# Spectral filter and Mish layer on one core: filter rows of both halves in one transfer, twelve DMA-transposed tiles in pairs, a new order

## The chip, the core and the metric

The kernel runs on one core of one Trainium2 chip. The core has a matrix engine (PE; its weight loads are shown as PEld), two elementwise engines (ACT, which is ScalarE, and DVE, which is VectorE), GpSimd (POOL) and SyncE (SP), which here only issues transfers (DMAs). Sixteen DMA engines move the data. The metric is the device time of one execution in microseconds (us).

## What is computed

The inputs are bf16. `x` has 2048 rows of 512; `B_x` is not used, both branches read the same `x`.

```python
g = sigmoid((x * gate_w).sum(-1))                 # one number a row
X = rfft2(x) * (A_w_r + 1j * A_w_i)               # filter: 2048 x 257
a = irfft2(X)                                     # 2048 x 512
h = x @ w1 + b1                                   # 512 -> 1792
b = (h * tanh(softplus(h))) @ w2                  # Mish, 1792 -> 512
out = g * a + (1 - g) * b
```

## The kernel before

The work is a list of named tasks. `_build` creates them with what they read and write, and the string `ORDER` gives every task's place: a token is the task's name, its engine and, for results in PSUM or in a temporary, the bank or slot. `_Graph.place` turns `ORDER` into one list for each engine and adds the waits; each engine then executes its list strictly in order. SP and ACT issue the DMAs that stand in their lists, also in order, and a DMA whose data is not there yet holds up all that stand behind it.

Rows of `x` are split in 16 tiles `t` of 128, and the tiles in four chunks `c` of 512 rows. These are the tasks, with the names that the texts use (line numbers are those of the kernel before):

- `x0`, `x2`, `x4`, `x8`, `x12` load `x` in five pieces (L515-516). `tr` transposes a tile on PE (L554), `evx` copies it out of PSUM into `xT`. Tiles 0 to 7 go this way; tiles 8 to 15 come transposed from DRAM by one DMA each, `xt8` to `xt15` (L533-534).
- `m{c}_{ft}` is the first matmul of the Mish layer: chunk `c`, 128 of its 1792 columns, four 512-wide matmuls (L800); `h{c}_{ft}` is its Mish on ACT (L805). The result of chunk 0 and 1 goes to `hs01`, of chunk 2 into `rD` and of chunk 3 into `rS`. So `h2` may not write `rD` before all eight DMAs `sh` have read it, and `h3` may not write `rS` before the filter has been read from there (`dph`, L791).
- `n{t}_..` is the second matmul of tile `t` (L828, 14 matmuls).
- The forward transform: `bf` sums and differences on DVE (L567), `p` on PE (L577) and its copy `ep`, `d` (L591) and its copy `ed` into `y1` in `rD`; then eight DMAs `sh0_0` to `sh1_3` (256 KB each) carry `y1` to `In` in `rE`. `sh0` needs `ed0` to `ed3`, `sh1` needs `ed4` to `ed7`. `t0` to `t7` transform `In` with the constants `ldM` (L676), with copies `et` into `Y`; `t0` to `t3` read `sh0`, `t4` to `t7` read `sh1`.
- The filter: the rows of `A_w_r` (`wr`) and `A_w_i` (`wi`) are loaded into the staging buffer `rS`. Each of the two has two halves of 32 frequencies: `wr0`, `wr1`, `wi0`, `wi1`. The plain rows of a half are one transfer of 16 rows of 16,448 bytes (`wr0s0`, 257 KB), its mirrored rows another (`s1`, 16 x 31 or 16 x 32 rows of 514 bytes), and a single row of the first half comes by itself (`s2`). `wrm`/`wim` copy from `rS` into the filter `rW` and `rA` (L638 to L641), `wrn` is a DMA that doubles the real part.
- `p2`, `p1`, `ad` on DVE multiply `Y` by the filter; `e1`, `xp`, `ead`, `e2`, `e3` treat the edge frequencies.
- The inverse transform: `it` (L750) with copies `eit`, eight DMAs `hx`, `id` (L774) with `ec` and `ey`, and `ip` (L812).
- `o` and `s` combine the branches (L817, L822), `out` DMAs store two tiles at a time; the last tile is cut at column 384.
- `gt` on DVE is the row sum for the gate, sixteen times 128x512 (L599).

The lines that make the filter's transfers and the transposing DMAs are these:

```python
parts = [(0, slice(0, 32), slice(32 * fh, 32 * fh + 32), 257), ...]      # plain rows of half fh
dma(f"{nm}{fh}s{j}", sg[pm:32:2, fs, :], wv[:, ms, :].rearrange("q m k -> q (m k)"), ...)
dma(f"xt{t}", xT[:, t // 4, :, t % 4, :], xv[:, t, :], queue=("sp",), transpose=True, ...)
```

Of the kernel before, what the change touches and what calls it, by code (L numbers as in the profile page):

```python
# [300 lines left out]
cRF:act ones:pool ident:pool ebase:pool x0:sp x2:sp w1_0a:sp warm:pe:0 fl0:pe:1  # L301
tr0:pe:0 gwl:act braw:act w1_0b:sp x4:sp bf0_0:dve bf0_1:dve tab:act w1_4:sp
x8:sp tr1:pe:1 evx1:act evx0:dve p0:pe:2 p1:pe tr2:pe:0 w1_9:sp x12:sp
wr0s1:sp wi0s2:sp wi0s0:sp wr0s2:sp cFD:sp wr0s0:sp ldM0:sp bf2_0:dve bf2_1:dve
tr3:pe:1 p2:pe:4 p3:pe tr_b:pe:6 evx3:dve ev_b:dve evx2:act fl1:pe:7 m0_2a:pe:1
m0_1a:pe:0 m0_1b:pe m0_2b:pe m0_3a:pe:6 m0_0a:pe:7 m0_3b:pe m0_0b:pe ep2:act ep0:dve
h0_2:act h0_1:act h0_3:act gwb:pe:0 bf4_0:dve bf4_1:dve tr4:pe:1 evx4:dve p4:pe:2
tr7:pe:6 p5:pe evx7:dve ep4:dve tr5:pe:4 m0_6:pe:1 tr6:pe:6 h0_0:act evx5:act
evx6:dve m0_8:pe:4 bf8_1:dve bf8_0:dve xt8:sp xt9:sp xt10:sp h0_8:act h0_6:act
gwe:act xt11:sp gt0:dve p6:pe:2 m1_8:pe:6 p7:pe p8:pe:4 p9:pe ep8:dve  # L310
ep6:act h1_8:act m0_7:pe:1 h0_7:act m1_7:pe:0 m1_5:pe:2 h1_5:act p10:pe:4 p11:pe
m1_0:pe:1 ep10:act h1_0:act bf12_1:dve bf12_0:dve gt1:dve p14:pe:2 p12:pe:6 p15:pe
p13:pe m1_4:pe:4 m0_4:pe:1 gt2:dve ep12:dve gt3:dve ep14:act d6:pe:2 d14:pe:6
gt4:dve h1_7:act h1_4:act h0_4:act ldM1:sp d7:pe gt5:dve d2:pe:4 d15:pe
ed3:act ed7:act d3:pe m1_12:pe:1 d4:pe:2 ed1:dve gt6:dve d5:pe m1_3:pe:0
ed2:dve h1_12:act h1_3:act d0:pe:4 d1:pe ed0:act m1_1:pe:1 sh0_2:sp sh0_0:sp
sh0_1:sp sh0_3:sp m1_2:pe:0 d10:pe:2 h1_2:act d12:pe:4 d13:pe h1_1:act m0_10:pe:6
d11:pe d8:pe:0 d9:pe h0_10:act ed4:act ed6:act wrm011:dve gt7:dve m2_6:pe:7
gt8:dve m1_13:pe:6 gt9:dve ed5:dve wrm000:dve gt10:dve m0_12:pe:0 m0_5:pe:1 m1_10:pe:4
gt11:dve gt12:dve t1_0:pe:2 wi0s1:sp sh1_2:sp sh1_3:sp sh1_0:sp sh1_1:sp h1_13:act  # L320
t1_1:pe m2_0:pe:6 h0_5:act wrm001:act et1:act m1_9:pe:1 m2_4:pe:5 h1_9:act gt13:dve
gt14:dve h0_12:act h1_10:act t0_0:pe:2 gt15:dve wip0:pool wip1:pool wim000:dve zcl:dve
t0_1:pe wi1s0:sp wr1s0:sp et0:act m0_9:pe:1 ez:pool wrm010:dve wr1s1:sp wi1s1:sp
m1_11:pe:0 wrp0:pool wrp1:pool m2_8:pe:4 h1_11:act h2_8:act wim011:dve wim001:dve wim010:dve
t3_0:pe:2 t3_1:pe et3:act h2_4:act h2_6:act m1_6:pe:0 m2_7:pe:4 h2_0:act h2_7:act
h0_9:act h1_6:act xt12:sp xt13:sp ez1:dve win0:dve wic0:dve wiz0:dve xt14:sp
xt15:sp wrn00:sp wrn01:sp t2_0:pe:2 t2_1:pe p20_0:dve:0 et2:dve wim110:dve m2_1:pe:5
m2_13:pe:7 h2_1:act h2_13:act ldM3:sp ldM2:sp m2_2:pe:4 m2_10:pe:1 w2_4:sp h2_10:act
h2_2:act wrm110:dve p22_0:dve:1 wim101:dve wrm101:act w2_0:sp w2_9:sp p23_0:dve:2 wim111:dve
wim100:dve wrm111:dve p22_1:dve m2_3:pe:5 m0_13:pe:7 m2_12:pe:4 m2_5:pe:6 m2_9:pe:1 p20_1:dve  # L330
m3_0:pe:0 wrn11:sp wrm100:act wrn10:sp win1:dve h0_13:act h2_12:act h2_3:act h2_9:act
h3_0:act m3_4:pe:2 m3_10:pe:7 m3_12:pe:3 m3_5:pe:1 m0_11:pe:0 m3_13:pe:5 wic1:dve wiz1:pool
wrc0:dve wrz0:dve p23_1:dve h2_5:act h3_4:act h3_5:act h3_10:act h3_12:act h3_13:act
m3_3:pe:1 m3_9:pe:3 t5_0:pe:4 h3_3:act h0_11:act t5_1:pe t4_0:pe:6 t4_1:pe m3_11:pe:2
t6_0:pe:0 t6_1:pe p1_3:dve p1_0:dve ad_0:dve et5:act et4:act h3_9:act m2_11:pe:4
m3_2:pe:5 p21_0:dve:0 h3_11:act p21_1:dve p1_1:dve p1_2:dve ad_2:dve t7_0:pe:2 m3_7:pe:6
t7_1:pe m3_1:pe:7 h2_11:act et6:act ad_3:dve omg:dve ad_1:dve p24_0:dve:1 p25_0:dve:0
p25_1:dve p26_0:dve:2 p24_1:dve p26_1:dve m3_6:pe:4 h3_7:act et7:act wrc1:dve wrz1:dve
n2_0:pe:6 n1_0:pe:2 gc:dve p1_6:dve p1_4:dve o1_0:act n6_0:pe:3 o6_0:act h3_1:act
# [12 lines left out]
ip11:pe:2 ip5:pe:4 id0:pe:6 id1:pe s15_384:dve n13_0:pe:5 ec8:act:0 s5:dve ey8_0:dve
ey8_1:dve ec0:act:1 out15_384:sp ey0_0:dve ey0_1:dve id2:pe:0 id3:pe ip10:pe:4 ip14:pe:6
o14:dve out5:sp n14_0:pe:7 o10:act o11:dve s11_0:dve s13_0:dve ip6:pe:6 n10_0:pe:5
ip1:pe:4 ec2:act:0 ey2_0:dve s14_0:dve ey2_1:dve ip3:pe:7 ip2:pe:0 ip9:pe:1 ip8:pe:3
n8_0:pe:2 s10_0:dve s1:dve s6:dve o9:act out11:act s3:dve s2:dve out3:act
ip7:pe:0 ip0:pe:1 o8:dve s0:dve s7:dve out1:act out7:act n9_0:pe:3 s9_0:dve
s8_0:dve out13:sp out14:sp out9:sp n15_0:pe:0 s15_0:dve out15_0:act
# [3 lines left out]
def _build(nc, A_x, A_w_r, A_w_i, B_x, B_w1, B_b1, B_w2, gate_w, out, XTP=8, LATE=8, NWARM=13, TRM=4,  # L362
# [10 lines left out]
    with es:  # L373
# [41 lines left out]
        xT = rX[:].rearrange("p (c a t m) -> p c a t m", c=NCH, a=4, t=4)  # L415
# [106 lines left out]
        for ri, (src, nm) in enumerate(((A_w_r, "wr"), (A_w_i, "wi"))):  # L522
            wv = src.rearrange("(q m) k -> q m k", m=128)
            for fh in range(2):
                sg = stg[64 * ri + 32 * fh:64 * ri + 32 * fh + 32]
                c0_ = 1 - fh
                parts = [(0, slice(0, 32), slice(32 * fh, 32 * fh + 32), 257),
                         (1, slice(31, 0, -1) if fh == 0 else slice(31, None, -1), slice(97, 128) if fh == 0 else slice(65, 97), 514)]
                if fh == 0:
                    parts.append((1, slice(0, 1), slice(64, 65), 8))  # L530
                for j, (pm, fs, ms, kb) in enumerate(parts):
                    dma(f"{nm}{fh}s{j}", sg[pm:32:2, fs, :], wv[:, ms, :].rearrange("q m k -> q (m k)"), kb=kb, writes=[(nm, fh, "s", j)])
        for t in range(XTP, NT):  # L533
            dma(f"xt{t}", xT[:, t // 4, :, t % 4, :], xv[:, t, :], queue=("sp",), transpose=True, kb=128, writes=[("xT", t)])
# [9 lines left out]
        for t in range(XTP):  # L544
            b = _Buf("b1")

            def f_tr(e, t=t, b=b):
                ins = None
                for dt_ in range(4):
                    xs = x_sb[:, t, 128 * dt_:128 * (dt_ + 1)]  # L550
                    if t < TRM:
                        ins = e.matmul(bank(b)[:, 128 * dt_:128 * (dt_ + 1)], xs, identt[:, :], start=True, stop=True)
                    else:
                        ins = e.transpose(bankb(b)[:, 128 * dt_:128 * (dt_ + 1)], xs, identt[:, :])  # L554
# [3 lines left out]
            evac(f"evx{t}", lambda t=t: xT[:, t // 4, :, t % 4, :], lambda b=b, t=t: (bank(b) if t < TRM else bankb(b)[:, 0:512]).rearrange("p (a c) -> p a c", a=4), 512, [b], [("xT", t)], "trm" if t < TRM else "tr")  # L558
        for t in range(XTP, NT):
# [230 lines left out]
        for c in range(NCH):  # L790
            dph = {0: [], 1: [], 2: t_sh, 3: t_mv}[c]  # L791
            for ft in range(NFT):
# [3 lines left out]
                for h in ((0, 1) if split else (2,)):  # L796
                    def f_mm1(e, c=c, ft=ft, b=b, h=h):
                        ins = None
                        for dt_ in (range(4) if h == 2 else range(2 * h, 2 * h + 2)):
                            ins = e.matmul(bank(b), w1_sb[:, dt_, 128 * ft:128 * (ft + 1)], xT[:, c, dt_, :, :], start=(dt_ == 0), stop=(dt_ == 3))  # L800
# [98 lines left out]
```

## Time and profile before

| | us |
|---|---|
| median of 3 runs (130.64 to 131.45) | 130.84 |
| the profiled execution | 130.94 |
| its span, from the first to the last instruction | 129.2 |
| outside the span | 1.7 |

The profile shows one execution. PE's clock was granted in full throughout. A row of the chain of waits or of the timeline begins with its start and its length in us; "x34" is how many instructions were merged into it. SPq and ACTq rows are issues of DMAs. The list of DMA issues has, last in each row, the median us from issue to landing. In the 40 slices each digit is the busy share of 3.2 us in tenths.

### The profile page before, as it was taken

The page shows a single profiled execution, that of the slowest core. Times are in us where ns is not written, and L with a number is a line of the kernel's source. Part 1 is how long each engine was busy: PE and PEld are TensorE (multiplying, and loading weights), DVE is VectorE, ACT ScalarE, POOL GpSimd, SP SyncE. Part 2 cuts the span into 40 slices and gives each one's busy share as a digit, 9 for nine tenths or more (in the row PEclk, how much of TensorE's full clock was granted, in tenths as well). Part 3 has the DMA queues.
Part 4 walks back from the last instruction along what each step waited for, and adds up shares of the span by engine and source line. Part 5 has one row for each costly group of instructions (what it writes and reads, how often), then busy time and mean ns, then how long its engine had stood idle before and what let it go on. Part 6 is the DMA issues. An engine that isn't in the chain of part 4 may idle for free.

```text
span 129.2 us, 2150 instructions
## 1 busy us (share of the span) xinstructions
PE 124.5 (96%) x841; PEld 68.1 (53%) x856; DVE 95.6 (74%) x164; ACT 71.8 (56%) x101; POOL 5.8 (5%) x13
## 2 busy tenths in 40 slices
PE   7999999999999999999999999998999999999992
PEld 5645656765555544346544447583556554544450
DVE  0748699999997999999799833463196679677851
ACT  3556689979799999999930275273015331302000
POOL 2000000000077000000000000000000000000000
PEclk9999999999999999999999999999999999999999
DMA  3999999919999999999159200004902002032243
GB/s 89 308 334 396 251 209 138 252 51 327 296 271 155 183 219 338 360 266 228 41 134 274 119 0 0 0 5 154 391 33 77 9 0 91 0 122 81 81 167 112
DMA packets 16759, 21.20 MB, mean 164 GB/s; under 512 B 5805, under 2 KB 11694, under 8 KB 16686
## 3 DMA queue, kind: packets, MB, share of 16 engines
q1 hardware_dynamic: 15280, 18.84, 55.8%
q10 hardware_dynamic: 1470, 2.23, 4.7%
q8 instruction: 7, 0.11, 0.4%
q14 instruction: 2, 0.02, 0.0%
HBM read 12.66 MB, written 2.10 MB: 114 GB/s over the span
## 4 chain that ended last, share of the span: by engine, by line
PE 88%; DMA 3%; ACT 3%; DVE 1%; ACTq 1%; issue 1%; SPq 0%
PE ps L800 36%; PE ps L828 35%; DMA rA<-in_A_x_dram 3%; PE ps L750 3%; PE ps L676 3%; PE ps L591 3%; PE ps L774 3%; PE ps L812 3%; PE ps L577 2%; ACTq L463 1%; ACT hs L805 1%; ACT rF L475 1%; PE ps L554 1%; ACT rC L475 1%; DVE rB L567 1%
## 5 line engine op out<-in xcount | busy, mean ns | idle before, releaser
L800 PE MATMUL ps<-rX,w_sb 128*128 128x512 bf16 x215 | 50.3, 379 | 0.5
L800 PEld LDWEIGHTS ps<-rX,w_sb 128*128 128x128 bf16 x224 | 20.7, 98 | 21.9 <-ACT rD L805 1.1
L828 PE MATMUL ps<-w_sb,hs 128*128 128x512 bf16 x109 | 24.9, 379 | 0.6 <-ACT rX L817 0.4
L805 ACT ACTIVATE hs<-ps,b1f 128x512 bf16<-128x512 f32 x28 | 18.4, 697 | 5.0 <-PE ps L800 4.9
L828 PEld LDWEIGHTS ps<-w_sb,hs 128*128 128x128 bf16 x112 | 10.8, 98 | 13.0 <-ACT rX L817 0.9
L828 PE MATMUL ps<-w_sb,rS 128*128 128x512 bf16 (+2 forms) x70 | 12.9, 336 | 0.0
L828 PE MATMUL ps<-w_sb,rD 128*128 128x512 bf16 x55 | 12.5, 379 | 0.1
L599 DVE SCALAR_TENSOR_TENSOR w_sb<-rA,w_sb 128x512 bf16<-128x512 bf16 x16 | 11.0, 688 | 1.4 <-ACT w_sb L475 1.0
L689 DVE TENSOR_TENSOR tmp<-rC,rA 64x1024 bf16<-64x1024 bf16 x16 | 10.7, 685 | 1.1 <-ACT rC L475 0.6
L475 ACT ACTIVATE rC<-ps 128x1024 bf16<-128x1024 f32 x11 | 11.2, 1034 | 0.3 <-PE ps L577 0.3
L817 ACT ACTIVATE rX<-ps,omg 128x512 bf16<-128x512 f32 x5 | 3.4, 687 | 13.7 <-PE ps L828 12.0
L784 DVE TENSOR_TENSOR rA<-tmp,ps 128x512 bf16<-128x512 f32 x16 | 10.1, 679 | 1.3 <-ACT tmp L475 1.2
L567 DVE TENSOR_TENSOR rB<-rA 128x1024 bf16<-128x1024 bf16 (+1 forms) x10 | 5.4, 580 | 5.7 <-DMA rA<-in_A_x_dram 5.5
L475 ACT ACTIVATE tmp<-ps 128x512 f32<-128x512 f32 x7 | 4.1, 595 | 9.6 <-PE ps L774 9.6
L828 PEld LDWEIGHTS ps<-w_sb,rS 128*128 128x128 bf16 x70 | 6.3, 98 | 5.6
L822 DVE SCALAR_TENSOR_TENSOR rX<-ps,omg,rX 128x512 bf16<-128x512 f32 (+2 forms) x9 | 6.0, 688 | 4.1 <-PE ps L828 4.0
L805 ACT ACTIVATE rD<-ps,b1f 128x512 bf16<-128x512 f32 x14 | 8.9, 717 | 0.3 <-PE ps L800 0.3
L805 ACT ACTIVATE rS<-ps,b1f 128x512 bf16<-128x512 f32 x14 | 8.8, 721 | 0.3 <-PE ps L800 0.3
L828 PEld LDWEIGHTS ps<-w_sb,rD 128*128 128x128 bf16 x56 | 5.5, 98 | 6.6 <-DVE rX L822 0.2
L817 ACT ACTIVATE rX<-ps,gcol 128x512 bf16<-128x512 f32 x4 | 2.6, 686 | 9.2 <-PE ps L812 6.2
L475 DVE CAST rF<-ps 128x1024 bf16<-128x1024 f32 x4 | 4.8, 1222 | 3.8 <-PE ps L750 3.8
L822 DVE SCALAR_TENSOR_TENSOR rX<-ps,gcol,rX 128x512 bf16<-128x512 f32 x8 | 5.6, 745 | 2.3 <-PE ps L812 2.3
(78 smaller groups left out, 132.3 us busy)
## 6 DMA issues: line engine op xcount, KB each, us to landing
w_sb<-in_B_w_dram SPq DMA_DIRECT2D x4, 640.0 KB, 9.6
rF<-c_m SPq DMA_DIRECT2D x4, 512.0 KB, 6.6
rE<-rD SPq DMA_DIRECT2D x8, 256.0 KB, 2.6
rB<-c_g SPq DMA_DIRECT2D x4, 512.0 KB, 6.4
rA<-in_A_x_dram SPq DMA_DIRECT2D x3, 512.0 KB, 9.1
rW<-rW SPq DMA_DIRECT2D x4, 260.0 KB, 7.5
rC<-rF ACTq DMA_DIRECT2D x4, 256.0 KB, 3.3
rC<-rF SPq DMA_DIRECT2D x4, 256.0 KB, 3.7
```

The lines of the kernel that those rows point to most:

```text
L475: fns = dict(dve=lambda e: e.tensor_copy(out=o(), in_=i()), act=lambda e: e.activation(o(), i(), AF.Copy))
L567: return e.tensor_tensor(out=xu[:, a:b_, uv, :], in0=x_sb[:, a:b_, 0:256], in1=x_sb[:, a:b_, 256:512], op=ALU.add if uv == 0 else ALU.subt ...
L591: ins = e.matmul(o[:, 2 * e_:2 * e_ + 2, uv, :], zu[:, c, g, :], FD[:, c, :].rearrange("p (r k) -> p r k", r=2), start=True, stop=True)
L599: t_gt.append(dve(f"gt{t}", "gate", "stt", 512, lambda e, t=t: e.scalar_tensor_tensor(out=junk, in0=x_sb[:, t, :], scalar=1.0, in1=gwr, op ...
L676: ins = e.matmul(bank(b, i)[:, 128 * k:128 * (k + 1)], Mm[:, f, :], In[:, _fin(f), :], start=True, stop=True)
L689: return e.tensor_tensor(out=zv(z)[lo], in0=Y[hi, f0:f0 + 8, :], in1=Wi[hi, f0:f0 + 8, 0:128], op=ALU.mult)
L784: return e.tensor_tensor(out=yb[:, t:t + 2, 256 * h:256 * h + 256].rearrange("p t (i e) -> p t i e", e=2), in0=t4(z), in1=o4(bank(b, 1)), ...
L800: ins = e.matmul(bank(b), w1_sb[:, dt_, 128 * ft:128 * (ft + 1)], xT[:, c, dt_, :, :], start=(dt_ == 0), stop=(dt_ == 3))
L805: G.add(f"h{c}_{ft}", "mish", dict(act=lambda e, c=c, ft=ft, b=b: e.activation(hs[c][:, ft, :], bank(b), AF.Mish, bias=b1f[:, ft:ft + 1])) ...
L817: f_a = lambda e: e.activation(o_()[0], o_()[1], AF.Copy, scale=o_()[2])
L822: dve(name, "fin", "psums", hi - lo, lambda e: e.scalar_tensor_tensor(out=bs[:, t, lo:hi], in0=bank(b)[:, 0:hi - lo], scalar=col[:, t:t + ...
L828: ins = e.matmul(bank(b)[:, 0:hi - lo], hs[c][:, ft, 128 * tl:128 * (tl + 1)], w2_sb[:, ft, lo:hi], start=(ft == 0), stop=(ft == NFT - 1))
```

## The change

- `XTP` falls from 8 to 4: tiles 4 to 15 are transposed by DMA, two tiles in one transfer of 256 KB (`xt4`, `xt6`, ... `xt14`), so there are six such DMAs instead of eight, and `tr4` to `tr7` with their copies are gone. The layout of `xT` becomes tile before column block; the first matmul reads it with that stride.
- The plain rows of both halves come in one transfer each, `wis0` and `wrs0`: on the SBUF side 32 partitions of 16,448 bytes, on the DRAM side a pattern of 2 x 16 rows of 16,448 bytes (the half is the outer count). The single rows become `wis2` and `wrs2` in the same way (2 x 16 rows of 514 bytes). The mirrored rows stay, now 31 in both halves.
- All outputs are issued by ACT. The last tile's 128 columns are computed last, where before the 384 were.
- `ORDER` is written anew: engines, banks and places. The gate's broadcast copy `gwe` goes to DVE and `ep0` to ACT; more `hx` go to SP; five `n` instead of four stand ahead of `it`.

```diff
-... XTP=8, LATE=8, NWARM=13, TRM=4,
+... XTP=4, LATE=8, NWARM=13, TRM=4,
-        xT = rX[:].rearrange("p (c a t m) -> p c a t m", c=NCH, a=4, t=4)
+        xT = rX[:].rearrange("p (c t a m) -> p c t a m", c=NCH, a=4, t=4)
+            wh = src.rearrange("(q a h f) k -> a h q f k", a=2, h=2, f=32)
+            sg = stg[64 * ri:64 * ri + 64]
+            dma(f"{nm}s0", sg[0:64:2].rearrange("p f k -> p (f k)"), wh[0].rearrange("h q f k -> h q (f k)"), kb=514, ...)
+            dma(f"{nm}s2", sg[1:64:2, 0, :], wh[1][:, :, 0, :], kb=16, ...)
             for fh in range(2):
-                parts = [(0, slice(0, 32), slice(32 * fh, 32 * fh + 32), 257), ...]
-                for j, (pm, fs, ms, kb) in enumerate(parts):
-                    dma(f"{nm}{fh}s{j}", sg[pm:32:2, fs, :], wv[:, ms, :].rearrange("q m k -> q (m k)"), kb=kb, ...)
-        for t in range(XTP, NT):
-            dma(f"xt{t}", xT[:, t // 4, :, t % 4, :], xv[:, t, :], queue=("sp",), transpose=True, kb=128, ...)
+                ms = slice(97, 128) if fh == 0 else slice(65, 96)
+                dma(f"{nm}{fh}s1", sg[32 * fh + 1:32 * fh + 32:2, 31:0:-1, :], wv[:, ms, :].rearrange("q m k -> q (m k)"), kb=249, ...)
+        for t in range(XTP, NT, 2):
+            dma(f"xt{t}", xT[:, t // 4, t % 4:t % 4 + 2, :, :].rearrange("p t a m -> p (t a) m"), xv[:, t:t + 2, :].rearrange("p t d -> p (t d)"),
+                queue=("sp",), transpose=True, kb=256, ...)
-                            ins = e.matmul(bank(b), w1_sb[:, dt_, 128 * ft:128 * (ft + 1)], xT[:, c, dt_, :, :], ...)
+                            ins = e.matmul(bank(b), w1_sb[:, dt_, 128 * ft:128 * (ft + 1)], xT[:, c, :, dt_, :], ...)
```

Of the new order these places matter to the prediction. The first is SP's list around the redistribution `sh` (the rows `rE<-rD`); `rS` rows are the filter's, `c_m` is `ldM`, and the transposes are `xt`. Before:

```order
L463 DMA rF<-c_m 128x2048
L463 DMA rE<-rD 128x1x1024 [waits s_dve,s_act]
L463 DMA rE<-rD 128x1x1024 x3
L463 DMA rS<-in_A_w_i_dram 16x31x257
L463 DMA rE<-rD 128x1x1024 [waits s_dve,s_act]
L463 DMA rE<-rD 128x1x1024 x3
L463 DMA rS<-in_A_w_i_dram 16x8224
L463 DMA rS<-in_A_w_r_dram 16x8224
L463 DMA rS<-in_A_w_r_dram 16x32x257
L463 DMA rS<-in_A_w_i_dram 16x32x257
L462 DMA_TRANSPOSE rX<-in_A_x_dram 128x4x128 x4
```

The same place in the changed kernel, where its rows are numbered one line lower in the code:

```order
L462 DMA rE<-rD 128x1x1024 x2
L462 DMA rS<-in_A_w_i_dram 32x1x257
L462 DMA rS<-in_A_w_i_dram 32x1x8224
L462 DMA rS<-in_A_w_r_dram 16x31x257
L462 DMA rS<-in_A_w_r_dram 32x1x257
L462 DMA rS<-in_A_w_r_dram 32x1x8224
L462 DMA rE<-rD 128x1x1024 [waits s_act,s_dve]
L462 DMA rE<-rD 128x1x1024 x3
L462 DMA rS<-in_A_w_r_dram 16x31x257
L461 DMA_TRANSPOSE rX<-in_A_x_dram 128x8x128 x2
```

The two merged transfers (`32x1x8224`) and three smaller ones now stand between the last of `sh0` and the first of `sh1`, where before stood only one transfer of mirrored rows.

The second is ACT's list around the first `h2`, the row that waits for all eight `sh`; `hs` rows are `h0` and `h1`, `rC` rows are `et`, `rD` rows are `h2`. Before:

```order
L475 ACTIVATE rC<-ps 128x1024 [waits s_pe]
L805 ACTIVATE hs<-ps,b1f 128x512 [waits s_pe]
L805 ACTIVATE rD<-ps,b1f 128x512 [waits d_sh1_1,d_sh1_0,d_sh1_2,d_sh0_3,d_sh1_3,d_sh0_2,s_pe,d_sh0_1,d_sh0_0]
L475 ACTIVATE rC<-ps 128x1024 [waits s_pe]
L805 ACTIVATE rD<-ps,b1f 128x512 x3
L805 ACTIVATE rD<-ps,b1f 128x512 [waits s_pe]
```

In the changed kernel:

```order
L474 ACTIVATE rC<-ps 128x1024 [waits s_pe]
L474 ACTIVATE rC<-ps 128x1024
L803 ACTIVATE rD<-ps,b1f 128x512 [waits d_sh1_1,d_sh1_0,d_sh1_2,d_sh0_3,d_sh1_3,d_sh0_2,s_pe,d_sh0_1,d_sh0_0]
L803 ACTIVATE rD<-ps,b1f 128x512
L803 ACTIVATE rD<-ps,b1f 128x512 [waits s_pe]
L803 ACTIVATE rD<-ps,b1f 128x512
L803 ACTIVATE rD<-ps,b1f 128x512 [waits s_pe] x2
L803 ACTIVATE rD<-ps,b1f 128x512
L636 ACTIVATE rA<-rS 32x16x129 [waits d_wi1s1,d_wis2,d_wis0,s_dve]
```

All copies `et` of `t0` to `t3` now stand ahead of the first `h2`, seven `h2` follow in a row, and a copy of the filter stands on ACT behind them.

More of the change, by code (lines that the diff above doesn't have):

```diff
@@ L300 @@
 ORDER = """
[L301 to L327, printed above, removed]
@@ L627, in _build @@
                 sg = stg[64 * ri + 32 * fh:64 * ri + 32 * fh + 32]
-                rd = [(nm, fh, "s", j) for j in range(3 - fh)]
+                rd = [(nm, fh, "s", j) for j in range(3)]
                 mv = []
```

108 lines of the change are left out of this document (65 added, 43 removed).

## The prediction

> **What bounds the kernel now.** I read the page's first two parts, then the chain of waits in order of time, then the timelines of SP and ACT and the list of DMA issues.
>
> ```profile
> PE 124.5 (96%) x841; PEld 68.1 (53%) x856; DVE 95.6 (74%) x164; ACT 71.8 (56%) x101; POOL 5.8 (5%) x13
> PE   7999999999999999999999999998999999999992
> DMA  3999999919999999999159200004902002032243
> GB/s 89 308 334 396 251 209 138 252 51 327 296 271 155 183 219 338 360 266 228 41 134 274 119 0 0 0 5 154 391 33 77 9 0 91 0 122 81 81 167 112
> PE 88%; DMA 3%; ACT 3%; DVE 1%; ACTq 1%; issue 1%; SPq 0%
> ```
>
> PE has no idle slice between the first and the last, and the chain lies on it for 88%. So a saving is worth only what it takes off PE's list, off the start or off the tail. Against that, every wait that holds PE's list up costs in full. The second thing to see is the DMA row: the sixteen engines are busy almost without a break up to slice 18, some 61 us. A transfer that comes late there has no slack behind it.
>
> The chain also gives PE's pace, free of overlap:
>
> ```profile
> 7.08 3.40 PE ps L800 x15
> 11.97 0.22 PE ps L554 x4
> 34.63 0.45 PE ps L676 x8
> 43.32 7.34 PE ps L800 x34
> 126.82 0.62 DVE rX L822
> ```
>
> A 512-wide matmul is 7.34 / 34 = 0.216 us, a 128-wide one 0.45 / 8 = 0.056 us, a transpose the same. The last PE work ends at 126.8.
>
> **The change, part by part.** *Transposes.* `tr4` to `tr7` are 16 of the 0.056 us rows: PE loses 0.9 us. Their copies lie on ACT and DVE beside other work and go for nothing. What was their cover goes too: before, `m1` could start as soon as tiles 4 to 7 were transposed on PE. Now `m1` needs `xt4` and `xt6`, and these queue behind `x12`. Two rows of DVE's timeline show when the third and the last piece of `x` (`x4`, `x12`) came, since `bf4` and `bf12` start on them:
>
> ```profile
> 9.78 1.29 DVE L567 TENSOR_TENSOR rB<-rA 128x1024 bf16<-128x1024 bf16 x2 [1.63 <-DMA rA<-in_A_x_dram]
> 17.94 1.29 DVE L567 TENSOR_TENSOR rB<-rA 128x1024 bf16<-128x1024 bf16 x2
> ```
>
> SP's first nine issues are the same in both kernels, so `x4` and `x12` come at the same times. In the new list PE can do, from the end of `bf4` at 9.78 + 1.29 = 11.1: six `m0` and eight `p`, 24 x 0.216 + 32 x 0.056 = 7.0 us, to 18.1. The next is `p14`, which needs `bf12` on DVE, 17.94 + 1.29 = 19.2. So PE waits 1.1 us there; before, `m1_0` stood in that place.
>
> *Issue of the pairs.* SP's own time for the transposes:
>
> ```profile
> 13.10 9.60 SPq L462 DMA_TRANSPOSE rX<-in_A_x_dram  x4
> 37.50 5.57 SPq L462 DMA_TRANSPOSE rX<-in_A_x_dram  x4
> ```
>
> A tile takes 1.4 us to issue where nothing holds it up, 2.4 us where the queue ahead is full. A pair should take 2.8 to 4.8. The four pairs begin at about 11 us, the second is out by 20.5 (it can't be out before `x12` and `wi1s1` drain), and lands at about 22. `m1_1` is reached at 24, so I cost this at nothing; if a pair took the 4.8 after 18 us, `xt6` would land at 25 to 26, and PE would wait 2.
>
> *Outputs and the tail.* The last `s` goes from 384 columns (0.62 above) to 128 columns, and its store from 96 to 32 KB:
>
> ```profile
> L822 DVE SCALAR_TENSOR_TENSOR rX<-ps,omg,rX 128x128 bf16<-128x128 f32 x1 | 0.4, 351 | 0.0
> out_dram<-rX ACTq DMA_DIRECT2D x1, 96.0 KB, 1.7
> out_dram<-rX SPq DMA_DIRECT2D x1, 32.0 KB, 1.5
> ```
>
> That is 0.27 + 0.2, so 0.5 us less. ACT issues the stores when it has nothing else left, so its issue time is covered.
>
> *The merged filter rows.* This is the term that decides. SP's list now has `sh0`, then `wis2`, `wis0`, `wr0s1`, `wrs2`, `wrs0`, then `sh1`. What a transfer costs depends on how many DMA engines share it. The list of DMA issues tells something of that:
>
> ```profile
> w_sb<-in_gate_w_dram ACTq DMA_DIRECT2D x1, 1.0 KB
> w_sb<-in_B_b_dram ACTq DMA_DIRECT2D x1, 3.5 KB
> rS<-in_A_w_i_dram SPq DMA_DIRECT2D x3, 257.0 KB, 6.4
> rE<-rD SPq DMA_DIRECT2D x8, 256.0 KB, 2.6
> ```
>
> The first two have no landing time, because the list only gives one where all sixteen engines reported. They are the only two whose outermost count (1 row; 14 rows) is not a multiple of 16. So the engines are given whole slices of the outermost count. The new transfers have an outermost count of 2 on the DRAM side: two slices, two engines, and each of these moves 16 rows of 16,448 bytes one after the other, where before every engine had one.
>
> The price of such a row: the GB/s row peaks at 396, that is 24.8 for one engine, and 16,448 bytes take 0.66 us. The other end is the same kind of transfer while it shares memory with others:
>
> ```profile
> 34.87 0.61 SPq L463 DMA_DIRECT2D rS<-in_A_w_i_dram  x1
> 35.52 1.25 SPq L463 DMA_DIRECT2D rS<-in_A_w_r_dram  x2
> rS<-in_A_w_i_dram SPq DMA_DIRECT2D x1, 257.0 KB, 3.8
> rS<-in_A_w_r_dram SPq DMA_DIRECT2D x1, 257.0 KB, 5.0
> ```
>
> They land at 38.7 and 40.5, so 1.8 us for one row an engine. I take 0.66, since two engines alone have the memory for themselves; 1.8 stays as the upper end. The lower end is nothing, if the transfer is spread after all (first rival).
>
> [...]
>
> *When.* PE reaches `d1` after 60 wide and 92 narrow matmuls and `gwb`: 6.9 (the first `m0`, one wide matmul ahead of 7.08) + 61 x 0.216 + 92 x 0.056 + 0.6 (the `m0` end at 10.5, `bf4` at 11.1) + 1.1 = 26.9. Then DVE's `ed0`:
>
> ```profile
> L475 DVE CAST rD<-ps 128x1024 bf16<-128x1024 f32 x3 | 3.7, 1220 | 0.1
> 27.60 2.63 SPq L463 DMA_DIRECT2D rE<-rD  x4
> L805 ACT ACTIVATE rD<-ps,b1f 128x512 bf16<-128x512 f32 x14 | 8.9, 717 | 0.3 <-PE ps L800 0.3
> L638 ACT ACTIVATE rW<-rS 32x2064 bf16<-32x2064 bf16 x3 | 5.6, 1914 | 0.0
> ```
>
> With the rest of the `gt2` (0.7) ahead of it `ed0` ends at 28.6. SP needs 2.63 / 4 = 0.66 us an issue; `sh0_3` goes out at 31.2 and lands 2.6 later, so the two engines are free for the filter at about 33.5. On each of them then stand 8 KB (`wis2`), 263 KB (`wis0`), 16 KB (`wr0s1`), 8 KB, 263 KB (`wrs0`) and 4 x 16 KB (their share of `sh1`), 624 KB, 25.2 us at 24.8 GB/s. Since a queue's transfers land in the order of issue (38.7 and 40.5 above), `sh1` lands at about 58.7.
>
> Who waits: ACT's first `h2` for all of `sh`. On ACT stand behind it six more `h2` and a copy of 1.9 us. PE needs ACT for free banks. Ahead of `m2_6`, which takes the first `h2`'s bank, PE has 136 wide and 144 narrow matmuls and `gwb`: 6.9 + 137 x 0.216 + 144 x 0.056 + 1.7 = 46.3. It would start there at 46.3, and starts when the first `h2` is done, 58.7 + 0.7 = 59.4: 13.1 us lost. ACT is then in arrear: seven more `h2`, which overlap to 8.9 / 14 = 0.64, and the copy take 6.4 us until the bank of the eighth matmul is free, in which PE has 7 x 0.86 = 6.0: another 0.4. The filter's copies on DVE start when `wrs0` lands, 57 instead of 45, and `ldM3`, `w2` and `wrn` move with the rest; all are delayed by less than PE is, so nothing is added.
>
> **Sum**, against the profiled execution (130.94, of which 129.2 is span; 0.1 above the median): 130.94 - 0.9 + 1.1 - 0.5 + 13.1 + 0.4 = 144.1. I forecast 144.1.
>
> **Rivals.** *The merged transfers are spread over sixteen engines.* For it speaks that the SBUF side has 32 partitions, and that the transfers with an outer count of 16 to 128 all show sixteen. Then `wis0` lands at 36, nobody waits, and the sum is 130.94 - 0.9 + 1.1 - 0.5 = 130.6, 129.8 to 131.6: not slower. The point from which it decides: the bytes ahead of `sh1` must be through in the 12.8 us between 33.5 and `m2_6`, 317 KB an engine; the two merged transfers with their single rows hold 1,085 KB, so five engines or more.
>
> *The pairs are late too.* If an issue of a pair is as slow as the 2.4 us a tile of the first row, and the filter rows are spread, `m1_1` waits 2 us, and `m3_7` at 51 for `xt14` 1 more: 133 to 135.
>
> *The two engines are slower.* At 1.8 us a row 32 rows take 58 us instead of 21, and the time is 180; at 1.0 us 155. Against it speaks that nothing else uses memory meanwhile.
>
> **How the numbers follow.** The forecast (two engines, 0.55 to 0.8 us a row; 139 to 150) has 0.72, the spread 0.17, the late pairs 0.06, the slower rows 0.05. The range needs 8 in 10: it leaves out the slower rows and the edges of the others and reaches down to the spread, 129.9 to 150. A measurement here tells about 1% from no change, 129.5 to 132.1. Faster comes from the low edge of the spread alone, 0.05; same is most of the spread, 0.11; slower is the rest, 0.84.
>
> **What would show it.** Right: `wis0` and `wrs0` without a landing time in the list; `sh1` landing near 59; ACT's first `rD` row near 59 after a long idle time; PE idle for some 13 us in one piece from about 46; the DMA row low there, at two of sixteen. The small terms: a PE gap of 1.1 us at 18 ahead of L575, a last DVE row of 0.35. Wrong: a landing time for 514 KB of a few us, and no gap on PE at 46. Then the first rival holds, or, if the gap is ahead of `m1` at 24, the second.

## The result, and the profile after

The changed kernel takes 153.22 us (median of 6 runs, 151.97 to 154.13), the kernel before 130.84 beside it: 1.170 times, 95% interval 1.164 to 1.175. The forecast was 144.1, with a range up to 150. Here and below, ratios and intervals leave disturbed runs out, so they can differ a little from the quotient of two medians. The profiled execution took 154.13, its span 152.5; the points below are reckoned against it.

The page of the changed kernel, engines, slices and chain:

```profile
PE 127.5 (84%) x840; PEld 68.2 (45%) x840; DVE 95.3 (63%) x163; ACT 68.2 (45%) x98; POOL 5.3 (3%) x13
...
PE   7899999999992000029999999999999999999994
...
PEclk9999999999999555555999999999999999999999
DMA  4999999496127691169996029800049000003083
...
PE 59%; DMA 25%; SPq 10%; DVE 3%; issue 1%; ACT 0%; ACTq 0%
```

The gap stands where it was forecast, from slice 12 on. The DMA row is at one or two tenths in slices 10 and 11 and again in 15 and 16, where two of sixteen engines move data, but not in between: from 45.4 us on the other engines move their share of `sh1` and what stands behind it. Two things are new beside that. The gap is longer, some 21 us instead of 13. And PE's clock falls to half in it, which the prediction doesn't mention.

The chain of waits from the merged transfer to the end of the gap:

```profile
32.55 6.53 DMA rS<-in_A_w_i_dram
39.07 5.66 SPq L462
...
47.24 19.24 DMA rE<-rD
...
66.79 0.70 ACT rD L803
...
67.53 15.72 PE ps L798 x60
```

`wis0` is issued at 32.55; SP then stands in the issue of `sh1_1`; the last `sh1`, issued at 47.24, lands 19.2 us later; ACT's first `h2` follows at 66.79 and `m2_6` at 67.53. PE's timeline has the wait itself (the window ends at 76 us):

```profile
67.53 8.81 PE L798 MATMUL ps<-rX,w_sb 128*128 128x512 bf16 x28 [20.82 <-ACT rD L803]
```

The last matmul ahead of the gap ended at 46.7, near the 46.3 that the prediction reckoned, so PE stands 20.8 us, not 13.1. SP's timeline shows how long its issues were held (a merged row gives the issue time of several):

```profile
35.03 12.83 SPq L462 DMA_DIRECT2D rE<-rD  x4
...
48.62 18.48 SPq L461 DMA_TRANSPOSE rX<-in_A_x_dram  x2
```

Four `sh1` took 2.5 us to issue before and take 12.8 now. The merged transfers have no landing time in the list, as forecast; DVE's timeline gives it, since its copies of the filter begin when `wis0` and `wrs0` are there:

```profile
52.27 0.70 DVE L639 TENSOR_SCALAR rA<-rS 32x2064 bf16<-32x2064 bf16 x1 [13.21 <-issue]
...
63.91 0.70 DVE L638 COPY rW<-rS 32x2064 bf16<-32x2064 bf16 x1 [5.72 <-DMA rS<-in_A_w_r_dram]
```

The clock is read from the table of stretches (the last three columns are granted clock, DMA share and GB/s):

```profile
40.00:45.00 5.00, 5.00 (x36) 2.75 (x35) 0.00 (x0) 4.22 (x6) 0.00 (x0) 1.00 0.12 39
45.00:50.00 5.00, 1.71 (x8) 0.59 (x6) 0.00 (x0) 0.00 (x0) 0.00 (x0) 0.89 0.76 209
...
65.00:70.00 5.00, 2.47 (x6) 0.88 (x7) 4.10 (x8) 3.21 (x6) 0.00 (x0) 0.50 0.83 144
70.00:75.00 5.00, 5.00 (x18) 2.04 (x17) 4.81 (x7) 3.56 (x4) 0.00 (x0) 0.72 0.96 271
```

0.89 over five us means half clock for the last 1.1 of them, from 48.9, 2.2 us after PE's last matmul; 0.72 means that it lasts until 72.8, 5.3 us after PE works again. Meanwhile a wide matmul takes twice its time, 0.427 us from start to start instead of 0.216: the 60 from 67.53 take 15.72 us, where 60 x 0.216 is 12.95. Leaving out a fall at the very end of a run, the half clock lasts 23.9 us here; in others with one such fall it is, as far as mean clock (0.987 to 0.923) and span tell, 3.4 (e9_four, e15_ports16), 10.2 (e4_fill), 13.7 (e12_four), 17.1 (e14_ports), 20.5 (e13_far) or 23.9 (e3_swap), each time a multiple of 3.41. It begins 2.2 us after the last matmul ahead of the gap here, and 2.5 in e4_fill.

What the two engines do is in the trace's records of single packets. These are rows of 16,448 bytes, start and duration in us, of the changed kernel; 37.3 to 44 is a stretch in which no other packet moves:

```
37.30 0.962   37.91 0.982   38.26 1.268   38.88 0.964
57.31 0.613   57.45 0.613   57.91 0.620   58.05 0.613
```

The 16 rows that start in that stretch take 0.62 to 1.27 us, 0.90 on the mean. The first row starts at 35.1, the last ends at 63.4: 28.3 us for 32 rows and some 32 KB of smaller pieces an engine.

### The profile page after: what moved, and what is told of

The parts are those of the page before. It is cut to its first block, busy times and chain, and to the rows that moved or that the text cites. A ratio compares the mean times of both kernels' runs of the same rounds, so it can differ in the third digit from the quotient of the medians.

```text
span 152.5 us, 2118 instructions
## 1 busy us (share of the span) xinstructions
PE 127.5 (84%) x840; PEld 68.2 (45%) x840; DVE 95.3 (63%) x163; ACT 68.2 (45%) x98; POOL 5.3 (3%) x13
## 4 chain that ended last, share of the span: by engine, by line
PE 59%; DMA 25%; SPq 10%; DVE 3%; issue 1%; ACT 0%; ACTq 0%
PE ps L826 32%; PE ps L798 17%; DMA rE<-rD 13%; SPq L462 10%; DMA rA<-in_A_x_dram 8%; DMA rS<-in_A_w_i_dram 4%; PE ps L748 2%; PE ps L772 2%; PE ps L810 2%; DVE rD L474 2%; PE ps L589 1%; PE ps L674 1%; DVE rB L565 1%; DVE w_sb L597 1%; PE ps L575 1%
## 5 line engine op out<-in xcount | busy, mean ns | idle before, releaser
L798 PE MATMUL ps<-rX,w_sb 128*128 128x512 bf16 x224 | 54.5, 393 | 21.0 <-ACT rD L803 20.8
L798 PEld LDWEIGHTS ps<-rX,w_sb 128*128 128x128 bf16 x224 | 21.6, 101 | 45.1 <-ACT rD L803 21.9
L803 ACT ACTIVATE hs<-ps,b1f 128x512 bf16<-128x512 f32 x28 | 17.8, 689 | 7.3 <-PE ps L798 7.3
L474 ACT ACTIVATE rC<-ps 128x1024 bf16<-128x1024 f32 x13 | 12.9, 1033 | 1.0 <-PE ps L674 0.8
L782 DVE TENSOR_TENSOR rA<-tmp,ps 128x512 bf16<-128x512 f32 x16 | 10.2, 683 | 4.5 <-ACT tmp L474 4.4
L826 PE MATMUL ps<-w_sb,rS 128*128 128x512 bf16 (+2 forms) x70 | 12.8, 336 | 0.0
L639 DVE TENSOR_SCALAR rA<-rS 32x2064 bf16<-32x2064 bf16 x3 | 2.1, 700 | 13.3 <-issue 13.2
L474 ACT ACTIVATE tmp<-ps 128x512 f32<-128x512 f32 x5 | 2.9, 594 | 14.7 <-PE ps L772 14.7
L638 DVE COPY rW<-rS 32x2064 bf16<-32x2064 bf16 x4 | 2.8, 696 | 6.4 <-DMA rS<-in_A_w_r_dram 6.4
```

Source lines behind the costliest of these rows:

```text
L474: fns = dict(dve=lambda e: e.tensor_copy(out=o(), in_=i()), act=lambda e: e.activation(o(), i(), AF.Copy))
L782: return e.tensor_tensor(out=yb[:, t:t + 2, 256 * h:256 * h + 256].rearrange("p t (i e) -> p t i e", e=2), in0=t4(z), in1=o4(bank(b, 1)), ...
L803: G.add(f"h{c}_{ft}", "mish", dict(act=lambda e, c=c, ft=ft, b=b: e.activation(hs[c][:, ft, :], bank(b), AF.Mish, bias=b1f[:, ft:ft + 1])) ...
L826: ins = e.matmul(bank(b)[:, 0:hi - lo], hs[c][:, ft, 128 * tl:128 * (tl + 1)], w2_sb[:, ft, lo:hi], start=(ft == 0), stop=(ft == NFT - 1))
```

## Experiments

Theory: the outermost count of 2 puts the merged transfers on two engines, `sh1` stands behind their rows in SP's queue, and PE waits for it. Rivals: the merging itself is slow, or another part of the change loses the time; and, for the excess over the forecast, where the 0.66 us a row went wrong.

**e1_split** undoes the merging alone: plain and single rows are one transfer for each half again, at the same places.

```diff
-wis2:sp wis0:sp ... wr0s1:sp wrs2:sp wrs0:sp
+wi0s2:sp wi1s2:sp wi0s0:sp wi1s0:sp ... wr0s1:sp wr0s2:sp wr1s2:sp wr0s0:sp wr1s0:sp
```

> The changed kernel with one part undone: the plain and the single rows come again as one transfer for each half (16 rows on the DRAM side), at the same place of SP's list; eight issues stand there instead of four. Theory (the merged transfers run on two DMA engines and hold up sh1 behind them, the rest of the change costs nothing): the 21 us gap on PE at 46 us goes, sh1 lands near 42, and the time is 130.6, 129.5 to 131.6. Rival (the new order or the paired transposes cause the wait): the gap stays at 10 us or more and the time is above 140.

132.31 us, 1.0101 times the time before (1.0063 to 1.0140). The gap is gone, the clock is full, and the merging is worth 20.9 us of the 22.4. But the rest of the change doesn't gain the 0.3 us of the sum, it costs about 1.4. PE's timeline of this kernel names two of the waits:

```profile
37.11 0.38 PE L675 MATMUL ps<-rE,rF 128*128 128x128 bf16 x4 [0.95 <-DVE w_sb L598]
...
48.34 1.90 PE L799 MATMUL ps<-rX,w_sb 128*128 128x512 bf16 x8 [1.51 <-ACT rD L804]
```

`t3_0` waits for `sh0_3`, which stands behind 512 KB of `ldM0` and lands at 36.8 (the row names an engine that was long done), and `m2_6` again waits for `sh1`, which stands behind the filter's rows and lands at 47.3.

**e2_outer16** keeps the merging and exchanges the outer counts, 16 x 2 instead of 2 x 16.

```diff
-            wh = src.rearrange("(q a h f) k -> a h q f k", a=2, h=2, f=32)
+            wh = src.rearrange("(q a h f) k -> a q h f k", a=2, h=2, f=32)
-... wh[0].rearrange("h q f k -> h q (f k)") ...
+... wh[0].rearrange("q h f k -> q h (f k)") ...
```

> The changed kernel with the merged transfers kept at the same size, the same 32 partitions and the same place, but with the DRAM side's two outer counts exchanged: 16 x 2 rows instead of 2 x 16. The plain and single rows land on other partitions of the staging buffer than they should, so the filter's values are wrong there; the work is the same. Theory (the outermost count gives the number of engines): both merged transfers have a landing time, sixteen engines share them, no gap, time 130.5, 129.5 to 131.6. Rival (merging itself, 32 partitions or 514 KB in one transfer, is slow): the gap stays, 145 or more.

132.88 us, 1.0122 times (1.0064 to 1.0180). The merged transfer now has a landing time in the list of its DMA issues:

```profile
rS<-in_A_w_i_dram SPq DMA_DIRECT2D x1, 514.0 KB, 7.5
rS<-in_A_w_r_dram SPq DMA_DIRECT2D x1, 514.0 KB, 9.6
```

So it is the outermost count and not the merging. Two further forms showed more of this by missing what they were made for. **e9_four** and **e11_halves** were to give four engines, and two engines whose rows lie far apart.

```diff
+            wq = src.rearrange("(g q a h f) k -> a g q h (f k)", g=4, a=2, h=2, f=32)   # e11_halves: g=2
-... wh[0].rearrange("h q f k -> h q (f k)") ...
+... wq[0] ...
```

> The changed kernel, with the 32 rows of wis0 and of wrs0 given in four groups of eight on the DRAM side (outermost count 4 instead of 2); the rows come to lie on other partitions of the staging tile, so the filter's values are not the reference's. Theory (the outermost count sets the number of engines, and those engines' rows hold sh1 up): four engines with 16 rows each. At the 0.84 us a row that the two engines took on the mean, the rows are through at about 50 instead of 63.4, sh1 lands at 51 to 52, PE stands some 6 us from 46.3, and with the clock's fall the time is 137; at 0.61 a row 133.5; so 133.5 to 139.5. Rival (fewer than sixteen engines is slow whatever their number, because SP's issue is blocked): 148 or more. Rival (it was the merging on the SBUF side after all): 152 to 154.

> The changed kernel, with the 32 rows of wis0 and of wrs0 divided between the two engines in another way: the first engine gets the first half of the tensor, the second the other half, 526 KB apart, instead of rows that are neighbours in DRAM; the rows come to lie on other partitions, so the filter's values are not the reference's. In the changed kernel rows of the two engines that start within 0.1 us of each other take 0.95 to 1.26 us, and 0.61 where they are shifted by 0.14 or more. If it is the neighbouring addresses that hamper each other, all rows now take 0.61 to 0.66, they are through at 56 to 57 instead of 63.4, and the time is 145 to 147. If it is the two engines themselves, or something else that works at the time, the first rows take 0.95 to 1.26 again, and the time is 152 to 156.

They came out at 1.0107 times (1.0067 to 1.0148) and, in a single run, at 134.39 us; all sixteen engines reported for `wis0` and `wrs0`, as in e2_outer16. The groups follow each other at the step of the rows, so the two counts fold into one of 16. In these two runs it was not the count written in the code that told, four or two, but the 16 that are left after folding.

**e12_four** has four groups that can't fold (other rows of the tensor).

```diff
+            wq = src.rearrange("(q c f) k -> c q (f k)", c=4, f=32)
-... wh[0].rearrange("h q f k -> h q (f k)") ...
+... wq[:, 0:8] ...
```

> The changed kernel, with an outermost count of 4 for wis0 and wrs0 that can't be folded into a longer one: four rows that are neighbours, times eight tensor rows. The last try at four groups had strides that fold into 16 equal steps, and the transfers landed like those of sixteen engines. Other rows of the tensor are read, so the filter's values are not the reference's. Theory (after folding, the outermost count is the number of engines, and those engines' rows hold sh1 up): wis0 and wrs0 have no landing time, four engines move 16 rows each; at the 0.84 us a row of the changed kernel's mean they are through at about 50, sh1 lands at 51 to 52, and the time is 137; at 0.61 a row 133.5; so 133.5 to 139.5. Rival (below sixteen engines it is as slow whatever their number): 148 or more.

147.26 us, 1.124 times (1.119 to 1.129). There is no landing time, and four engines reported. PE's timeline:

```profile
43.78 3.19 PE L799 MATMUL ps<-rX,w_sb 128*128 128x512 bf16 x14
61.08 3.17 PE L799 MATMUL ps<-rX,w_sb 128*128 128x512 bf16 x7 [14.12 <-ACT rD L804]
```

The wait is shorter than with two engines, 14.1 against 20.8, but it isn't halved: the time misses the 133.5 to 139.5. Between 37 and 46 a row takes 0.96 to 1.75 us, 1.35 on the mean, more than with two engines. So the price of a row isn't a constant; what it hangs on was still open.

**e3_swap** put `wrs0` first and `wis0` last.

```diff
-wis2:sp wis0:sp ... wr0s1:sp wrs2:sp wrs0:sp
+wrs2:sp wrs0:sp wr0s1:sp wis2:sp wis0:sp
```

> The changed kernel with the merged transfer of the real part ahead of that of the imaginary part on SP's queue, the mirrored rows wr0s1 between them as before, so that their landing marks the end of the first and sh1's the end of the second. In the changed kernel the first took some 17 us (about 1.0 us a row), the second 10 us (0.6 a row). If the first is slow because of its place in time (compute engines and other transfers are active until 46 us): wr0s1 lands at 52 to 54 and sh1 at 64 to 67 again, time 153. If the imaginary part's rows or their partitions 64 to 127 are slow: wr0s1 lands near 46 and sh1 at 64 to 67, time about 153 too.

A single run: 156.81 us. The rows of `wrs0`, now first, take 0.86 to 1.26 us from 35.4 to 46, those of `wis0`, now second, 0.61 to 0.66 from 54.5 on. So it is neither tensor.

**e13_far** leaves two engines but lets them read halves that lie 526 KB apart.

```diff
+            wq = src.rearrange("(g z f) k -> g z (f k)", g=2, f=32)
-... wh[0].rearrange("h q f k -> h q (f k)") ...
+... wq[:, 0:16] ...
```

> The changed kernel, still with an outermost count of 2, but the two engines read halves of the tensor that lie 526 KB apart, instead of rows that are neighbours, and each engine's rows follow each other without gaps; other rows of the tensor are read, so the filter's values are not the reference's. If the two engines' rows hamper each other by neighbouring addresses, all rows that move alone now take 0.61 to 0.66 us, the last is through at 56 to 58 instead of 63.4, and the time is 145 to 148. If the addresses play no part, the first rows take 0.95 to 1.26 again where no other packet moves, and the time is 152 to 157. Either way wis0 and wrs0 have no landing time, and the gap at 46 stays.

A single run: 153.49 us. The rows between 37.3 and 41, with no other packet, still take up to 1.27, so neighbouring addresses in DRAM are not the cause. What the forms with two engines share is the other side: row n of the first engine goes to partition 2n of its tensor's share, row n of the second to 32 + 2n.

**e14_ports** changes that side: every fourth of 128 partitions, so the two engines are 64 apart. The filter's copies wait for both tensors (not in the lines below).

```diff
-            dma(f"{nm}s0", sg[0:64:2].rearrange("p f k -> p (f k)"), ...
+            dma(f"{nm}s0", stg[2 * ri:128:4].rearrange("p f k -> p (f k)"), ...
```

> The changed kernel, with the same reads in DRAM, still two engines, but the rows of wis0 and wrs0 written to every fourth of all 128 partitions instead of every second of 64: the two engines' rows then lie 64 partitions apart at each step, where in the changed kernel they lie 32 apart. The filter's copies wait for both transfers, and the filter's values are not the reference's. Theory (rows that go to partitions 32 apart at the same time share one way into SBUF: 2 x 0.613 = 1.23 us when they are in step, 0.613 when they have drifted apart): all rows that move alone take 0.61 to 0.62 from the first on, the last is through at 56 to 57 instead of 63.4, sh1 lands at 58.5 to 60, and the time is 146 (145 to 147.5). Rival (the partitions play no part): 0.95 to 1.26 again in the first half, 152 to 155.

The packet records in the stretch without other packets, to set beside those of the changed kernel:

```
37.24 0.613   37.73 0.613   37.85 0.613   38.34 0.613
41.39 0.620   41.52 0.613   42.01 0.613   42.13 0.613
```

From 37.2 to 42.6 every row takes 0.613 or 0.620, where the changed kernel had 0.62 to 1.27. The rows are through at 59.0, 24.2 us after the first started, against 28.3. So 4.1 us go to two engines that write partitions 32 apart at the same time. In the changed kernel they drift apart, one ends 1.7 us or almost three rows ahead of the other, and get in each other's way no longer, hence the 0.613 at the end; in e14_ports they stay within about one row of each other and have 0.613 even so. The step of each engine's own rows also went from two partitions to four; with a step of two the changed kernel reaches 0.613 too, so the step is not the cause. e12_four fits: its four engines lie 16 partitions apart, so two pairs lie 32 apart; that wasn't tried by itself.

The rest of the forecast missed. While the other engines move `sh1` (42.6 to 48), a row takes 0.73 to 1.1; `sh1` lands at 62.8 and not by 60. And this kernel's copies of the filter wait for both tensors:

```profile
63.87 6.51 PE L798 MATMUL ps<-rX,w_sb 128*128 128x512 bf16 x21 [17.84 <-ACT rD L803]
```

PE goes on 3.7 us earlier than in the changed kernel, but waits 1.3 us again ahead of `m3_5`, to which the late copies come through ACT. The time is 151.06 us, 1.154 times (1.150 to 1.157), instead of 146.

**e15_ports16** makes the same change in the sixteen-engine form.

> The form with the outer counts exchanged (sixteen engines, 132.9), with the same change of the partitions: every fourth of 128 instead of every second of 64. The filter's copies wait for both transfers, and the filter's values are not the reference's. [...]

1.0294 times (1.0214 to 1.0373). It missed the author's estimate of 131 to 132.3 us, which no run bears out: `wis0` lands 2.9 us behind `wis2`, not 1.2 to 1.4 (2.42 in e2_outer16), and `sh1` at 48.0, where it was 48.4. The rows' mean did fall, from 1.35 us in e2_outer16 to 1.18, but the landings hardly moved, so with sixteen engines something else sets them. What it is stays open. The time is longer because the chain of waits now runs through the copies that wait for both tensors; the profiled execution also has 3.4 us at half clock.

**The clock.** **e4_fill** gave PE 350 narrow matmuls on constants between `m2_7` and `m2_6`, into a bank that is free.

```diff
-FILL = (1, 2)
+FILL = (1, 2, 350)
-m2_7:pe:6
+m2_7:pe:6 fl2:pe:7
```

> The changed kernel with 350 matmuls of 128 columns on constants into the free bank 7 behind m2_7, 19.5 us of PE work that fills most of the gap; nothing else is moved. Theory (in the gap PE's clock falls to half, and the slow matmuls after it cost 2.5 us): the clock stays full, the time falls by 2 to 2.8 us to about 150.7. Rival (after the gap ACT's arrears hold PE, not the clock): within 0.7 us of 153.2.

161.03 us, 1.228 times (1.222 to 1.234): slower by 8 instead of faster. The stretches tell why, with the row of PE's waits:

```profile
60.00:64.00 4.00, 2.57 (x44) 2.39 (x41) 0.00 (x0) 0.00 (x0) 0.00 (x0) 1.00 0.11 47
64.00:68.00 4.00, 0.00 (x0) 0.00 (x0) 2.77 (x5) 0.59 (x2) 0.00 (x0) 0.63 0.23 52
68.00:72.00 4.00, 1.46 (x14) 1.46 (x15) 3.70 (x7) 2.41 (x5) 0.00 (x0) 0.50 1.19 186
```

```profile
PE ps L497 <- issue: 8.0, 1, 8.0
```

The matmuls wait for no data, yet PE stops from 62.6 to 70.5, after 270 of the 350. The packet records show a 16,384-byte packet of the instruction queue at 68.2, just after the last row (64.1) and `sh1` (67.1). The likely reading is that PE had run out of instructions; the records don't tell which engine the packet was for, though what was expected of e5_fill512 takes it as given. The rest ran until 77.5, mostly at half clock. So it was no test of the clock. That the packet stood behind the rows fits the order of the records, but wasn't tried by itself.

**e5_fill512** gives the same time to 90 matmuls of 512 columns.

```diff
-FILL = (1, 2)
+FILL = (1, 2, 90)
-                    ins = e.matmul(bank(fb)[:, 0:128], one, one, start=True, stop=True)
+                    ins = e.matmul(bank(fb)[:, 0:m], one, wide[:, 0:m], start=True, stop=True)   # m = 512
```

> The changed kernel, with 90 matmuls of 512 columns on constants, into a PSUM bank that is free there, on PE between m2_7 and m2_6; the output stays as it is. 350 narrow ones had kept PE at work only to 62.8, where PE stood 7.8 us until its next 16 KB of instructions came at 68.2, behind the last row of the merged transfers, and then ended only at 77.3. 90 wide ones take 90 x 0.216 = 19.4 us, 46.3 to 65.8, with a quarter of the instructions. Theory (the clock is a term of its own): the clock stays at 1.00, the 60 matmuls from m2_6 on take 12.95 us instead of 15.72, and the time falls from 153.2 to 150.4 (149.5 to 151.4). Rival (the fall of the clock costs nothing, ACT or the transfers set the pace there anyway): 153 to 154. Rival (PE runs out of instructions here too): a stop of PE that nothing but issue ends, and 154 or more.

The clock stays full, and the same 60 matmuls in the chain:

```profile
68.13 13.21 PE ps L801 x60
```

13.21 us instead of 15.72: the clock is worth 2.5. The time is 152.18, 1.156 times (1.149 to 1.164) against 1.170, so 1.8 us less. It missed 151.4; in its profile `sh1` landed 0.6 us later, which is part of that. The rivals fell: the fall of the clock costs time, and nothing stopped PE.

**Another place.** **e6_actq** issued the four merged transfers from ACT, **e7_behind** put `sh1`, `xt12` and `xt14` ahead of them on SP.

```diff
-wis2:sp wis0:sp ... wrs2:sp wrs0:sp                       # e6_actq
+wis2:act wis0:act ... wrs2:act wrs0:act
-wis2:sp wis0:sp ... sh1_1:sp sh1_3:sp sh1_2:sp sh1_0:sp ... xt12:sp xt14:sp      # e7_behind
+sh1_1:sp sh1_3:sp sh1_2:sp sh1_0:sp xt12:sp xt14:sp wis2:sp wis0:sp ...
```

> The changed kernel, with the four merged transfers (wis2, wis0, wrs2, wrs0) issued by ACT at the same places of the list, the rest by SP. If sh1 was late because it stands in the same queue behind the rows of the two engines, it now lands at about 40 to 44, PE has no gap at 46, and the time is 133 to 137 (the split form's 132.3, 2.4 us of issue on ACT, and the late filter rows). If the two engines take one packet from each queue in turn, each of sh1's 32 packets on an engine waits for a row of 0.6 to 1.0 us, sh1 lands after 60 again, and the time is 148 to 154.

> The changed kernel, with sh1, xt12 and xt14 issued ahead of the merged filter rows instead of behind them. Theory (the gap at 46 is sh1 behind the rows, nothing else): sh1 lands at about 38 to 41, PE has no gap at 46.3. The filter is late instead: its last row is through at 62 to 68, ACT waits for wis0 at its first copy of the filter, DVE for wrs0, and e1, which came 35 us after the rows in the split form, comes at 97 to 103: 145 to 152 in all. Rival (the two engines are as slow whatever stands behind, but the filter has slack): 133 to 140. The price of a row: if the first 16 rows took 0.95 us because SP stood with a blocked issue (sh1_1, 9.7 us) on the same engines, they now take about 0.62 where no other packets move; if it is what else works at that time (ACT, PE, DVE), 0.95 again.

A single run each: 156.85 and 163.54 us, both slower than the changed kernel. In both, `sh1` lands by 43.1 and 39.4, and PE has no gap at 46, so it was the place behind the rows. But ACT reached its issues only at 39.9, after `sh1` was issued, so e6_actq says nothing on how two queues share an engine. Where the time goes instead is on PE's timeline of e7_behind:

```profile
43.69 8.80 PE L798 MATMUL ps<-rX,w_sb 128*128 128x512 bf16 x40
64.15 4.09 PE L798 MATMUL ps<-rX,w_sb 128*128 128x512 bf16 x12 [11.66 <-ACT rD L803]
85.67 4.87 PE L798 MATMUL ps<-rX,w_sb 128*128 128x512 bf16 x11 [17.43 <-ACT rS L803]
```

First ACT stands at its copy of `wis0`, then `h3` waits for DVE, whose work waits for `wrs0`. From the end of the last row to `e1` it took 35.9 us here, 34.7 in e6_actq, 36.4 in e1_split and 37.9 in the changed kernel. So in the changed kernel the filter was only some 2 to 3 us from being the bound too, and the two later places cost more than they saved; a place ahead of `sh0` wasn't tried.

**A better order.** **e8_order** and **e10_order2** are e1_split with `sh1` ahead of `wr` and `m0_5` ahead of `p14`, and with `ldM0` elsewhere.

```diff
-... ldM0:sp sh0_0:sp sh0_3:sp ... wr1s0:sp ... sh1_1:sp sh1_3:sp sh1_2:sp sh1_0:sp
+ldM1:sp ldM0:sp wi0s1:sp ... sh0_0:sp sh0_3:sp ... sh1_1:sp sh1_3:sp sh1_2:sp sh1_0:sp wr0s1:sp ...    # e8_order
+... sh0_0:sp sh0_3:sp ldM0:sp ... sh1_1:sp sh1_3:sp sh1_2:sp sh1_0:sp wr0s1:sp ...      # e10_order2
```

> The form with split filter rows (132.3), with three moves in the order: ldM0 is issued right behind ldM1 instead of between sh0_2 and sh0_0; sh1 is issued ahead of the four transfers of wr instead of behind them; m0_5 stands ahead of p14. Theory: what the split form loses to the kernel before are three waits of PE on its list, 1.3 us ahead of t3_0 (sh0_3 behind ldM0's 512 KB), 1.9 ahead of m2_6 (sh1 behind the filter rows) and 0.6 ahead of p14; without them 132.3 - 3.8 = 128.5 (127.8 to 129.5), below the kernel before. Rival (the waits only move: ACT, DVE or the filter's later rows end the same stretch): 130.5 to 132.5.

> The form of 130.65 us (split filter rows, sh1 ahead of wr, m0_5 ahead of p14), with ldM0 issued right behind sh0_3 instead of ahead of wi0s1. There all four sh0 took 6 to 7 us to land, behind ldM1, ldM0 and wi0s1, and t3_0 waited for sh0_3 until 37.1. Theory: the sixteen engines are full from 25 to 45, and only the order of the bytes is free; sh0_3 now lands at about 34, t3_0 doesn't wait, and sh1 lands a little later than the need for it: 129.6 (129.0 to 130.3), 1% below the kernel before. Rival (the filter rows of wr end the same stretch, since ACT and DVE wait for them at 47): 130.4 to 131.2, as without the move.

0.9961 times (0.9936 to 0.9986) and 1.0040 (1.0017 to 1.0062). Neither reached its 128.5 or 129.6. In e10_order2 PE has no wait at `t3_0` or `m2_6` any more:

```profile
PE   7999999999999997999999999999999999999994
```

Its longest wait on data is now ahead of `m3_7`, the first to need `xt14`, which lands at 51.8:

```profile
PE ps L799 <- DMA rX<-in_A_x_dram: 1.2, 1, 1.2
```

Beside that, its first wide matmul starts 0.6 us later than in e1_split. So without the merging the change is worth less than half a per cent, one order a little faster than the kernel before, the other a little slower.

## Why the prediction was wrong, point by point

- *The mechanism* was right, each step: two engines (e2_outer16), `sh1` behind their rows (e1_split, e7_behind), ACT's first `h2`, PE's gap from 46.7, forecast for 46.3. The first rival, spread over sixteen engines, fell.
- *The price of a row* is the step that failed, "I take 0.66, since two engines alone have the memory for themselves". The end value was nearly right, 0.613. But the engines weren't alone: they had each other. With partitions 32 apart, a row took 0.62 to 1.27 before the two had drifted apart, 0.90 on the mean, and with `sh1` moving beside it up to 1.4. Instead of 32 x 0.66 and 1.3 for the small pieces, 22.4 us, it was 28.3: 5.9 of the error. e14_ports gives 4.1 of it to the partitions. The range's low end of 0.55 a row is shown by no run: the fastest rows took 0.613. The third rival, 1.0 us a row, had a chance of 0.05 and the argument "nothing else uses memory meanwhile"; that looked at DRAM and not at the other end of the transfer. Its 155 lies nearest to the measured time, but in part by luck: the rows took (28.3 - 1.3) / 32 = 0.84 us, not 1.0, and a later start and the clock, which it left out, made up the rest.
- *When the rows start*: at 35.1 instead of 33.5 (31.2 + 2.6 is 33.8; the prediction went on with 33.5). `sh0_3` landed at 36.7 and not 2.6 us after its issue at 31.2. The prediction took the landing time of the kernel before, where nothing large was on its way any more; here 512 KB of `ldM0` had just been issued. 1.6 us.
- *From the last row to* `m2_6`: 4.1 us instead of 3.5. With the two points above this makes the 8.1 by which `m2_6` was late against its 59.4.
- *The clock* was left out, a term put at nothing without a reason. The sum had 0.4 for ACT's arrears; it was 15.72 - 12.95 = 2.8, of which e5_fill512 shows 2.5 to be the clock.
- *The wait ahead of* `p14`, 1.1 in the sum, was 0.34 by PE's timeline; it lies ahead of `m2_6`, whose start the rows set, so it changed nothing. The *transposes* and *pairs* were right: `xt6` landed at 22.5, and `m1_1` ran at 24.2 without a wait. Issues of the first four pairs took 1.3 to 4.5 us.
- *The tail* was right: from PE's last work to the end 1.86 us instead of 2.34, 0.5 less, with a last DVE row of 0.35.
- *The filter's copies* added nothing, as said, but by a margin of only some 2 to 3 us (e6_actq, e7_behind).

The late `m2_6`, 8.1, and the clock with the arrears, 2.8 - 0.4 = 2.4, make 10.5; between 144.1 and 154.13 lie 10.0. Where 0.5 came back behind `m2_6` was not traced.

## What to carry to other kernels

Count how many engines a transfer gets from its folded outermost count before merging two transfers into one: with a count of 2 the same rows took 28.3 us from the first to the last, with 16 (e2_outer16) 9.3, and the queue behind them stood. When two engines move long rows, look at both ends: rows on partitions 64 apart instead of 32 took 0.613 us each where nothing else moved, though the form with sixteen engines landed hardly earlier. A long gap on PE costs more than its length, so a forecast of a gap needs that term: in these runs every gap of 8 us or more was followed by half clock, as were those of 2.1 in e9_four and 2.3 in e15_ports16 (mean clock 0.987 in both), and none of up to 1.9 was (e5_fill512, at 1.000). Whether every gap between 1.9 and 8 us is, they don't show. Behind the gap of 21 us it cost 2.5.

## What the runs showed that was not expected

- Rows written at the same time to partitions 32 apart took up to 1.27 us, to partitions 64 apart 0.613, with nothing else moving.
- With 16,448-byte rows on two engines, PE stopped after 270 of 350 small matmuls and stood 8.0 us, it seems for lack of instructions; with 90 large ones it didn't stop.
- SP's issue of a 256 KB transfer, 0.6 us otherwise, was held for up to 10 us, and that of a pair of transposes for 15, while two of sixteen engines were behind.
